# Tap division ahead of the input folds, rotation angles first on ScalarE's queue, batch 1's folds from step 8, ScalarE's side work behind the seed

## The chip, the cores and the metric

The kernel runs on one core of a Trainium2 chip. The metric is the device time of one execution in microseconds; the figure for a kernel is the median of several runs.

## The reference

A Fourier mixing of the input is followed by a gated feed-forward block with a convolution of three taps along the sequence. All is fp32 in effect; the weights come as 8-byte floats.

```
X   = real(fft(fft(x, axis=1), axis=2))          # x: 8 x 3136 x 256
h   = max(X @ w_in, 0)                           # w_in: 256 x 1024
c   = w0 * h[s-1] + w1 * h[s] + w2 * h[s+1]      # conv_w: 3 x 1024, zeros past the ends
out = (h * sigmoid(c)) @ w_out                   # w_out: 1024 x 256
```

## The kernel before

**Setup.** The transform along the sequence uses its symmetries: VectorE folds each batch of x, which comes in two halves (`xh[b, 0]` and `xh[b, 1]`), in eight operations a half (`fold_ops`: `pair(0)`, `pair(2)`, `both(6)`, `feats(1)`, `both(4)`, `turned`, `evens`, `feats(0)`) into the tile w. Part of the odd frequencies is rotated: ScalarE scales by angles in the tile `turn` (`scaled`, L217 for batch 0 and L221 for the others), and for batches 1 to 7 VectorE finishes it (`turned`, L227). For batch 0 the rotated parts are products of their own. TensorE multiplies the folded x by cosine and sine tables (`tabs`, tile tab) in units of one PSUM bank; for each unit ScalarE copies a part (`Unit.copy`, L350, L380, L404) and VectorE combines it (`Unit.fin`). The result is PQ (tiles pt and qt). The transform along the features is multiplied into w_in ahead of time: `blocks` and `column` make G and ge.

The 8-byte weights are narrowed to fp32 by integer operations on VectorE (`narrow`, L618 to L636): conv_w and the first block of w_in at the start, the other blocks of w_in and w_out during the first steps, where a part of it goes to ScalarE (L620).

`taps()` transposes the narrowed conv_w on TensorE, lets ScalarE copy it out of PSUM (L736), and divides the outer taps by the middle one on VectorE (L738 to L744), so that the middle tap needs no product: it is put back as the scale of the sigmoid. In program order it stands right ahead of batch 0's folds.

**Order of the loads.** Loads go out on SyncE's and ScalarE's queues, and the mirrored rows of x by indirect DMAs on POOL (L132). On ScalarE's queue stand conv_w, single rows of x (L126), the four small DMAs of the angles (`load_turn`, L287), and, behind the negation of the angles (L699), one half of the odd tables (L274 to L279). The loads of both queues share eight semaphores in turn, so that each load also waits until the eighth one before it in program order has landed.

**Steps.** After the start the kernel walks through 256 steps (b, c, f): eight batches, four column chunks, eight blocks of 128 of the 1024 columns. The order is written out by hand (`manual_schedule`); all engines take their instructions in that order. In step t:

- ScalarE: `sigmoid` of step t-3 (L835), `copies` of step t+1 (L796), side work listed under "act", `keep`, `seed` of step t+2 (the constant part of h written into PSUM, L760), `first_tap` of t (L811).
- VectorE: `combine` of t (h from two PSUM products, L805), side work "dve", `last_tap` of t-2 (L820), its half of `gate` of t-3 (L844).
- POOL: the other half of `gate` (L843), `middle` of t (an accumulating DMA that adds h to the taps, L815), side work "pool" and the gathers of x under "load".
- TensorE: `products` of t+1 (pb and pa), `mm2` of t-4 (the product with w_out, po), side work "pe".

Side work is put in by `at(step, where, function)`. w_out is narrowed in steps 3, 5, 7 and 9. The features' column sums of batches 1 to 7 are done in steps 11 to 18 (`Feature`: three table operations on ScalarE under "act" in steps 11 to 13, then four stages). The units of batch 1 start at step 21. The 16 fold operations of batch 1 go to the list `cs`, which holds the free steps from 4 on: 4, 6, 8, 10, 11, 12, 13, 14, 16, 17, ... 23. The scaling for the rotation is put into the step of its `turned`, under "act". The loads of batch 2's first half follow batch 1's eighth fold operation.

PE is kept warm by products of no use (`keep_on`, the tile pb at the start) until the tables' products begin.

Of the kernel before, what the change touches and what calls it, by code (L numbers as in the profile page):

```python
# [9 lines left out]
F32 = mybir.dt.float32  # L10
# [3 lines left out]
ALU = mybir.AluOpType  # L14
# [19 lines left out]
TINY = 1e-18  # L34
# [3 lines left out]
def kernel(  # L38
# [10 lines left out]
    nc = tc.nc  # L49
    B, S, D = x.shape  # L50
    F = moe_w_in.shape[1]
    P = 128
# [9 lines left out]
    NF = F // P  # L62
# [6 lines left out]
    const = ctx.enter_context(tc.tile_pool(name="const", bufs=1))  # L69
# [17 lines left out]
    vt = nc.vector.tensor_tensor  # L87
    gt = nc.gpsimd.tensor_tensor
    stt = nc.vector.scalar_tensor_tensor
    act = nc.scalar.activation  # L90

    def mm(o, l, r, start, stop):
        nc.tensor.matmul(o, l, r, start=start, stop=stop, skip_group_check=True)  # L93

    def spare():

        return pso.tile([P, 2, D], F32, name="po", tag="po").rearrange("p a d -> p (a d)")
# [12 lines left out]
    def load_ops(b, h, eng, other=None, held=False):  # L110


        def plain():
            t = xp.tile([P, 8, 2, D], F32, name="xh", tag="xh")
            xh[b, h] = t
            if held:

                nc.gpsimd.memset(t[0:1, 0, 0, 0:1], 0.0)
            eng.dma_start(out=t[0:NP, 0:4], in_=bass.AP(
                tensor=x.tensor, offset=x.offset + (b * S + 1 + 2 * h) * D,  # L120
                ap=[[HQ * D, NP], [Q4 * D, 4], [1, 2 * D]]))

        def zero():
            t = xh[b, h]
            for s0, n, r in ((0, 4, 0), (4, 3, 1), (7, 1, 0)):
                (other or eng).dma_start(out=t[NP:KR, s0:s0 + n], in_=bass.AP(  # L126
                    tensor=x.tensor, offset=x.offset + (b * S + r * Q4) * D,
                    ap=[[D, 1], [Q4 * D, n], [0, 2], [1, D]]))

        def mirrored(m):  # L130
            def f():
                nc.gpsimd.indirect_dma_start(  # L132
                    out=xh[b, h][0:NP, 7 - m].rearrange("p q d -> p (q d)"),
                    out_offset=None,
                    in_=bass.AP(tensor=x.tensor, offset=x.offset,
                                ap=[[2 * D, B * S // 2], [1, 2 * D]]),
                    in_offset=bass.IndirectOffsetOnAxis(ap=idx[0:NP, 0:1], axis=0),
                    element_offset=(b * S + (4 - m) * Q4 - HO + 2 * (1 - h)) * D)
            return f
        return [plain] + [zero] * h + [mirrored(m) for m in range(4)]  # L140
# [142 lines left out]
    def load_turn(eng):  # L283

        for s in range(2):
            for i in range(2):
                eng.dma_start(out=turn[i:NP:2, s].unsqueeze(2), in_=bass.AP(  # L287
                    tensor=dft_seq.tensor, offset=dft_seq.offset + ((2 + s) * NQ + HQ * i) * HE,
                    ap=[[4 * NQ * HE, NP // 2], [2 * HE, 2], [1, 1]]))
# [349 lines left out]
    class Weight:  # L639
# [19 lines left out]
        def narrow(self, c0, c1):  # L659
# [5 lines left out]
    ident = gp.tile([3 * NF, 3 * NF], F32, name="ident", tag="g")  # L665
    make_identity(nc, ident)
    cw24 = gp.tile([3 * NF, 1, P], F32, name="cw24", tag="g")
# [6 lines left out]
           for tag in ("pt", "qt")]  # L674
    w_cv = Weight(cw24, moe_conv_w.rearrange("k (m p) -> (k m) p", m=NF).unsqueeze(1),
                  lambda sh: gp.tile(sh, I32, name="raw", tag="g"))
# [6 lines left out]
    def raw_in(i):  # L683
        def f(sh):
            if i % 2 == 0:
                raws[i // 2] = wp.tile([P, 2, *sh[1:]], I32, name="raw", tag="w%d" % (i // 2))
            return raws[i // 2][:, i % 2]
        return f

    w_in = [Weight(w4[i], moe_w_in[:, i * N4:(i + 1) * N4].rearrange("(t p) n -> p t n", p=P), raw_in(i))  # L690
            for i in range(4)]
    w_cv.load(nc.scalar)
    w_in[0].load(nc.sync)
    for h in range(2):
        for f in load_ops(0, h, nc.sync, nc.scalar, h == 1):
            f()

    load_turn(nc.scalar)
    act(turn[0:NP, 2], turn[0:NP, 1], AF.Copy, scale=-1.0)  # L699
    nc.gpsimd.memset(tabs[0][0:1, 0, 0, 0:1], 0.0)  # L700
    nc.gpsimd.memset(tabs[1][0:1, 1, 0, 0:1], 0.0)
# [7 lines left out]
    wout = const.tile([P, NF, D], F32, name="wout")  # L709
    G = const.tile([P, 2, F], F32, name="G")  # L710
    ge = const.tile([P, NF], F32, name="ge")
    cw = const.tile([P, 3, NF], F32, name="cw")

    def blocks(i):

# [14 lines left out]
                mm(p[:, m:m + 1], w[:, t, m * P:(m + 1) * P], dm[:, t, 1, P - 1:P], t == 0, t == 1)  # L730
        nc.scalar.copy(out=ge[:, i * NF // 4:(i + 1) * NF // 4], in_=p[:, 0:NF // 4])

    def taps():
        p = spare()
        mm(p[:, 0:3 * NF], cw24[:, 0], ident, True, True)
        nc.scalar.copy(out=cw.rearrange("p k m -> p (k m)"), in_=p[:, 0:3 * NF])  # L736
        small = const.tile([P, NF], F32, name="small")
        vt(small, cw[:, 1], cw[:, 1], op=ALU.mult)  # L738
        nc.vector.tensor_scalar(out=small, in0=small, scalar1=TINY * TINY, scalar2=2.0 * TINY, op0=ALU.is_lt,
                                op1=ALU.mult)  # L740
        vt(cw[:, 1], cw[:, 1], small, op=ALU.add)
        nc.vector.reciprocal(out=small, in_=cw[:, 1])
        for k in (0, 2):
            vt(cw[:, k], cw[:, k], small, op=ALU.mult)  # L744


    rows = out.rearrange("b s d -> (b s) d")
# [2 lines left out]
    def cut(s):  # L750
        b, c, f = s
        ch = chunks[c]
        return ch, ch.k1 - ch.k0, slice(f * P, (f + 1) * P)

    def seed(s):

        b, c, f = s
        ch, n, fs = cut(s)
        pa[s] = psa.tile([P, 512], F32, name="pa", tag="pa")
        act(pa[s][:, 0:n], eb[b, c], AF.Copy, scale=ge[:, f:f + 1])  # L760
# [15 lines left out]
    def products(s):  # L776
        b, c, f = s
        ch, n, fs = cut(s)
        pb[s] = psb.tile([P, 512], F32, name="pb", tag="pb")
        mm(pb[s][:, 0:n], G[0:P - 1, 1, fs], PQ[b][1][0:P - 1, ch.k0:ch.k1], True, True)  # L780
        mm(pa[s][:, 0:n], G[:, 0, fs], PQ[b][0][:, ch.k0:ch.k1], False, not triple(s))
        if triple(s):
            mm(pa[s][:, 0:n], G[0:P - 1, 1, fs], PQ[b][1][0:P - 1, ch.k0:ch.k1], False, True)
# [29 lines left out]
    def middle(s):  # L813
        n = gs[s].shape[1]
        nc.gpsimd.dma_start(out=gs[s], in_=hs[s][:, 1:1 + n], accum_op=ALU.add)  # L815
# [15 lines left out]
    def sigmoid(s):  # L831

        v, p, r = shares(s)
        for c in (slice(p.start, r.stop), v):
            act(gs[s][:, c], gs[s][:, c], AF.Sigmoid, scale=cw[:, 1, s[2]:s[2] + 1])  # L835
# [35 lines left out]
        gs.pop(s)  # L871


    w_cv.narrow(0, 1)
    w_in[0].narrow(0, 2)
    taps()
    idle = psb.tile([P, 512], F32, name="pb", tag="pb")

    def keep_on(banks):
# [9 lines left out]
    ops, _, pres = fold_ops(0)  # L889
# [34 lines left out]
    p = psd.tile([P, 512], F32, name="pd", tag="pd")  # L924
# [13 lines left out]
    taken = set()  # L938

    def at(cycle, where, fn):  # L940
        side.setdefault((cycle, where), []).append(fn)
# [16 lines left out]
    ends = [9, 23, per + 12] + [per * (b - 1) - 3 + max(11 - 4 * (b - 2), 0) for b in range(3, B)]  # L958
    def free(cycle):

        while cycle in taken:
            cycle += 1
        taken.add(cycle)
        return cycle
# [13 lines left out]
    for b in range(1, B):  # L978
# [6 lines left out]
        cs = [c0 + i * n // len(us) for i in range(len(us) + 1)]  # L985
        for i, u in enumerate(us):
            k = cs[i + 1] - cs[i]
# [8 lines left out]
    for b in range(1, B):  # L996
        ops, singles, pres = fold_ops(b)
        c0, n = ends[b - 1], ends[b] - ends[b - 1]
        if b == 1:

            cs = [c for c in range(4, ends[1] + 1) if c not in taken]
            assert len(cs) == len(ops) and cs[len(ops) // 2] > NF + 4
        else:
            cs = [free(c0 + j * n // len(ops)) for j in range(len(ops))]
            assert cs[-1] < ends[b]
        if b + 1 < B:
            for h in range(2):
                for j, fn in enumerate(load_ops(b + 1, h, nc.sync)):
                    at(cs[len(ops) // 2 * (h + 1) - 1] + 1 + j, "load", fn)
        for j, fn in enumerate(ops):  # L1010
            at(cs[j], "dve", fn)
        for j, fn in singles.items():
            at(cs[j], "pool", fn)
        for j, fn in pres.items():
            at(cs[j], "act", fn)
# [11 lines left out]
    for t in range(n + LAG):  # L1027
        def run(where):
            for fn in side.get((t, where), []):
                fn()  # L1030
        if 0 <= t - 3 < n:
            sigmoid(steps[t - 3])
        run("first")
        if t + 1 < n:
            products(steps[t + 1])
            copies(steps[t + 1])
        run("act")
        if t >= LAG:
            keep(steps[t - LAG])
        if t < n:  # L1040
            combine(steps[t])
        if t + 2 < n:
            seed(steps[t + 2])
        if t < n:
            first_tap(steps[t])

        run("dve")
        if 0 <= t - 2 < n:
            last_tap(steps[t - 2])
        if 0 <= t - 3 < n:  # L1050
            gate(steps[t - 3])
        if t + 1 < n:
            row_of(steps[t + 1])
        if t < n:
            middle(steps[t])
        run("pool")
        run("load")
        if t >= LAG:
            mm2(steps[t - LAG])
        run("pe")  # L1060
# [66 lines left out]
```

## Time and profile before

| | |
|---|---|
| median of 3 runs | 1190.13 us (1189.02 to 1190.2) |
| the profiled execution | 1192.42 us |
| its span, first to last instruction | 1190.7 us |
| granted TensorE clock, mean | 0.998 |
| PE busy | 1138.7 us (96%) |
| PEld busy | 888.1 us (75%) |
| DVE busy | 957.9 us (80%) |
| ACT busy | 945.0 us (79%) |
| POOL busy | 600.7 us (50%) |

PE is TensorE's matmuls, PEld its weight loads, DVE VectorE, ACT ScalarE, POOL GpSimd, SP SyncE; a q behind the name is the engine's queue of DMA issues and waits. Lines such as L93 are lines of the kernel before; L93 is the helper through which all matmuls go, so these are told apart by their tiles. Matmuls are pipelined and their ends modelled. An idle time is put down to the wait that ended last.

### The profile page before, as it was taken

Reading aid. Unit: us, or ns where it says so; the run is one execution under the profiler, and the core shown is the slowest. Engines: PE = TensorE matmul, PEld = TensorE weight load, DVE = VectorE, ACT = ScalarE, POOL = GpSimd, SP = SyncE. Lnnn points to the kernel's source line nnn. Section 1 sums busy time; section 2 is a strip of 40 time slices with the busy share of each in tenths; the row PEclk is TensorE's granted clock in tenths of the full one; section 3 lists DMA queues with packets and bytes.
Section 4 is the critical chain, followed back from the end, with each engine's and each line's share of the span. In section 5 each row is a group of like instructions: output and inputs, shape, how many; then the busy total and the mean of one; then the engine's idle time right before and its main releaser. Section 6 shows DMA issues by size and latency. Waiting matters only on the chain.

```text
span 1190.7 us, 16046 instructions
## 1 busy us (share of the span) xinstructions
PE 1138.7 (96%) x4818; PEld 888.1 (75%) x4818; DVE 957.9 (80%) x1448; ACT 945.0 (79%) x1939; POOL 600.7 (50%) x734
## 2 busy tenths in 40 slices
PE   0989899999999999999999999999999999999998
PEld 0656678778777787777778777777777777777776
DVE  3689878988788798988787788998787687787774
ACT  0388777887888788888787888888887888898885
POOL 4335765666364546565646464454444444444443
PEclk9999999999999999999999999999999999999999
DMA  7386696767587667767766576765566556666664
GB/s 200 107 153 134 144 161 159 154 139 156 118 193 148 144 122 169 159 149 154 160 137 138 120 173 141 168 142 122 120 124 123 120 121 137 132 131 129 125 122 103
DMA packets 107586, 168.15 MB, mean 141 GB/s; under 512 B 32657, under 2 KB 62627, under 8 KB 107501
## 3 DMA queue, kind: packets, MB, share of 16 engines
q0 software_dynamic: 41984, 115.83, 51.4%
q1 hardware_dynamic: 64345, 50.89, 15.0%
q8 instruction: 38, 0.62, 0.2%
q10 hardware_dynamic: 1172, 0.43, 0.2%
q14 instruction: 47, 0.39, 0.1%
HBM read 38.40 MB, written 25.74 MB: 54 GB/s over the span
## 4 chain that ended last, share of the span: by engine, by line
PE 79%; ACT 7%; DVE 6%; issue 4%; POOL 2%; DMA 2%; ACTq 0%; POOLq 0%; DVEq 0%; SPq 0%
PE po L93 50%; PE pb L93 12%; PE pa L93 11%; PE pd L93 6%; ACT g L835 2%; DVE g L820 2%; ACT nb L796 2%; POOL xh L132 1%; DMA g<-h 1%; ACT os L868 1%; ACT g L811 1%; DMA out_dram<-os 1%; ACT pa L760 1%; DVE xh L168 0%; DVE g L844 0%
## 5 line engine op out<-in xcount | busy, mean ns | idle before, releaser
L93 PE MATMUL po<-wout,g 128*128 128x256 f32 x3072 | 707.2, 380 | 11.1 <-DVE g L844 10.5
L93 PEld LDWEIGHTS po<-wout,g 128*128 128x128 f32 x3072 | 580.1, 190 | 158.2 <-DVE g L844 28.1
L815 POOL DMA_DIRECT2D g<-h x256 | 228.1, 891 | 470.2 <-ACT g L811 244.7
L835 ACT ACTIVATE g<-g,cw 128x385 f32<-128x385 f32 (+2 forms) x512 | 292.0, 623 | 86.6 <-DVE g L820 85.7
L820 DVE SCALAR_TENSOR_TENSOR g<-h,cw,g 128x770 f32<-128x770 f32 (+1 forms) x256 | 299.1, 1168 | 41.7 <-DMA g<-h 41.6
L843 POOL TENSOR_TENSOR g<-g,h 128x385 f32<-128x385 f32 (+1 forms) x256 | 292.7, 1143 | 54.9 <-ACT g L835 53.8
L796 ACT ACTIVATE nb<-pb 128x386 f32<-128x386 f32 (+3 forms) x512 | 226.6, 497 | 93.9 <-PE pb L93 93.3
L805 DVE CUSTOM_DVE_ANT_0 h<-pa,nb 128x386 f32<-128x386 f32 (+3 forms) x512 | 264.2, 556 | 15.7 <-POOL h L774 11.4
L811 ACT ACTIVATE g<-h,cw 128x770 f32<-128x770 f32 (+1 forms) x256 | 244.0, 953 | 0.0
L93 PE MATMUL pb<-qt,G 127*128 127x387 f32 (+2 forms) x512 | 213.9, 499 | 2.3 <-ACT nb L796 1.3
L93 PE MATMUL pa<-pt,G 128*128 128x387 f32 (+2 forms) x512 | 211.9, 494 | 1.7 <-ACT pa L760 1.7
L844 DVE TENSOR_TENSOR g<-g,h 128x385 f32<-128x385 f32 (+1 forms) x256 | 172.9, 675 | 17.9 <-ACT g L835 17.9
L760 ACT ACTIVATE pa<-eb,ge 128x387 f32<-128x387 f32 (+2 forms) x256 | 155.0, 606 | 3.8 <-DVE h L805 3.5
L93 PEld LDWEIGHTS pa<-pt,G 128*128 128x128 f32 x512 | 96.8, 189 | 75.8 <-issue 16.5
L132 POOL DMA_INDIRECT xh<-in_x_dram,idx x64 | 94.8, 1481 | 18.7 <-issue 13.4
L93 PE MATMUL pd<-tab,w 98*128 98x197 f32 (+2 forms) x448 | 98.2, 317 | 1.0 <-POOL w L181 1.0
L93 PEld LDWEIGHTS pb<-qt,G 127*128 127x128 f32 x512 | 90.8, 190 | 8.6 <-ACT nb L796 2.3
L93 PEld LDWEIGHTS pd<-tab,w 98*128 98x128 f32 (+1 forms) x448 | 82.0, 191 | 10.4 <-POOL w L181 1.4
L868 ACT COPY os<-po 128x256 f32<-128x256 f32 x196 | 57.7, 393 | 7.9 <-PE po L93 4.5
L157 DVE TENSOR_TENSOR xh<-xh 98x1020 f32<-98x1020 f32 (+1 forms) x32 | 47.6, 1492 | 0.0
L168 DVE TENSOR_TENSOR xh<-xh 98x1024 f32<-98x1024 f32 (+1 forms) x32 | 44.8, 1400 | 0.1
L227 DVE SCALAR_TENSOR_TENSOR w<-w,turn,rt 98x256 f32<-98x256 f32 x28 | 12.6, 491 | 25.3 <-ACT rt L221 21.3
(140 smaller groups left out, 425.1 us busy)
## 6 DMA issues: line engine op xcount, KB each, us to landing
g<-h POOLq DMA_DIRECT2D x192, 385.0 KB, 4.0
g<-h POOLq DMA_DIRECT2D x64, 416.0 KB, 4.2
out_dram<-os SPq DMA_DIRECT2D x192, 128.0 KB
xh<-in_x_dram SPq DMA_DIRECT2D x16, 784.0 KB
eb<-ed SPq DMA_DIRECT2D x16, 193.5 KB
raw<-in_moe_w_in_dram SPq DMA_DIRECT2D x4, 512.0 KB
raw<-in_moe_w_out_dram SPq DMA_DIRECT2D x1, 2048.0 KB
eb<-ed SPq DMA_DIRECT2D x8, 209.0 KB
```

The costliest lines, as they stand in the source:

```text
L93: nc.tensor.matmul(o, l, r, start=start, stop=stop, skip_group_check=True)
L132: nc.gpsimd.indirect_dma_start(out=xh[b, h][0:NP, 7 - m].rearrange("p q d -> p (q d)"), out_offset=None, in_=bass.AP(tensor=x.tensor, offs ...
L760: act(pa[s][:, 0:n], eb[b, c], AF.Copy, scale=ge[:, f:f + 1])
L796: act(nb[s][:, i, cols], p[:, cols], AF.Copy, scale=-1.0 if i else 1.0)
L805: nc.vector._custom_dve(TENSOR_ADD_SAT, out=to, in0=a[:, cols], in1=c[:, i, cols], s0=BIG, s1=0.0)
L811: act(gs[s], hs[s][:, 0:n], AF.Copy, scale=cw[:, 0, s[2]:s[2] + 1])
L815: nc.gpsimd.dma_start(out=gs[s], in_=hs[s][:, 1:1 + n], accum_op=ALU.add)
L820: stt(out=g, in0=h[:, k:k + n], scalar=cw[:, k, f:f + 1], in1=g, op0=ALU.mult, op1=ALU.add)
L835: act(gs[s][:, c], gs[s][:, c], AF.Sigmoid, scale=cw[:, 1, s[2]:s[2] + 1])
L843: gt(g[:, p], g[:, p], h[:, p], op=ALU.mult)
L844: vt(g[:, v], g[:, v], h[:, v], op=ALU.mult)
L868: nc.scalar.copy(out=osb[:, j % 2], in_=pt[:, j % 2])
```

## The change

Four things are done:

- `load_turn` goes ahead of conv_w on ScalarE's queue, which makes the angles its first load.
- conv_w and the first block of w_in are narrowed and `taps()` is called right behind the first loads. VectorE's and TensorE's order stays as it was (only line numbers move); on ScalarE the copy of the taps now stands ahead of the negation of the angles and of the odd tables' DMAs.
- The 16 fold operations of batch 1 go to a list of steps written out: 8, 10 to 14, 14, 16, 16, 17 to 23. The second half keeps its steps. The POOL copies, the scalings and the loads of batch 2's first half that go with the fold operations move with them.
- In each step `run("act")` moves from ahead of `keep` to behind `seed`, for all batches.

```diff
+    cw = const.tile([P, 3, NF], F32, name="cw")
+
+    def taps():
+        p = spare()
+        mm(p[:, 0:3 * NF], cw24[:, 0], ident, True, True)
+        nc.scalar.copy(out=cw.rearrange("p k m -> p (k m)"), in_=p[:, 0:3 * NF])
...
+    load_turn(nc.scalar)
     w_cv.load(nc.scalar)
     w_in[0].load(nc.sync)
     for h in range(2):
         for f in load_ops(0, h, nc.sync, nc.scalar, h == 1):
             f()
 
-    load_turn(nc.scalar)
+    w_cv.narrow(0, 1)
+    w_in[0].narrow(0, 2)
+    taps()
     act(turn[0:NP, 2], turn[0:NP, 1], AF.Copy, scale=-1.0)
...
-    w_cv.narrow(0, 1)
-    w_in[0].narrow(0, 2)
-    taps()
     idle = psb.tile([P, 512], F32, name="pb", tag="pb")
...
-            cs = [c for c in range(4, ends[1] + 1) if c not in taken]
-            assert len(cs) == len(ops) and cs[len(ops) // 2] > NF + 4
+            cs = [8, 10, 11, 12, 13, 14, 14, 16, 16, 17, 18, 19, 20, 21, 22, 23]
+            assert len(cs) == len(ops) and cs[-1] <= ends[1] and not taken & set(cs)
...
-        run("act")
         if t >= LAG:
             keep(steps[t - LAG])
         if t < n:
             combine(steps[t])
         if t + 2 < n:
             seed(steps[t + 2])
+        run("act")
         if t < n:
             first_tap(steps[t])
```

More of the change, by code (lines that the diff above doesn't have):

```diff
@@ L691 @@
             for i in range(4)]
+    cw = const.tile([P, 3, NF], F32, name="cw")
[3 more added lines that the diff above has]
+        nc.scalar.copy(out=cw.rearrange("p k m -> p (k m)"), in_=p[:, 0:3 * NF])
+        small = const.tile([P, NF], F32, name="small")
+        vt(small, cw[:, 1], cw[:, 1], op=ALU.mult)
+        nc.vector.tensor_scalar(out=small, in0=small, scalar1=TINY * TINY, scalar2=2.0 * TINY, op0=ALU.is_lt,
+                                op1=ALU.mult)
+        vt(cw[:, 1], cw[:, 1], small, op=ALU.add)
+        nc.vector.reciprocal(out=small, in_=cw[:, 1])
+        for k in (0, 2):
+            vt(cw[:, k], cw[:, k], small, op=ALU.mult)
+    load_turn(nc.scalar)
     w_cv.load(nc.scalar)
@@ L711 @@
     ge = const.tile([P, NF], F32, name="ge")
-    cw = const.tile([P, 3, NF], F32, name="cw")
     def blocks(i):
@@ L731, in column @@
         nc.scalar.copy(out=ge[:, i * NF // 4:(i + 1) * NF // 4], in_=p[:, 0:NF // 4])
[L733 to L744, printed above, removed]
     rows = out.rearrange("b s d -> (b s) d")
```

## The prediction

> **What bounds the kernel now.** I read the page first, then the busy time in stretches that follow the kernel's stages, then the waits, then the order of time of the first 42 us and of the first steps. The page's span, and the stretches (length, then PE, PEld, DVE, ACT and POOL busy with instruction counts, granted clock, DMA share, GB/s):
>
> ```profile
> span 1190.7 us, 16046 instructions
> ...
> 0.00:29.10 29.10, 0.59 (x2) 0.53 (x3) 11.10 (x26) 1.67 (x3) 12.47 (x29) 1.00 0.79 197
> 29.10:42.20 13.10, 11.19 (x29) 5.86 (x29) 12.74 (x17) 5.47 (x15) 4.44 (x7) 1.00 0.35 109
> ...
> 81.20:112.00 30.80, 28.09 (x111) 20.85 (x112) 30.59 (x52) 24.48 (x46) 14.87 (x25) 1.00 0.57 111
> 112.00:132.00 20.00, 16.59 (x68) 11.54 (x66) 15.06 (x22) 17.48 (x52) 12.19 (x15) 1.00 0.77 172
> ...
> 500.00:1000.00 500.00, 499.86 (x2128) 395.66 (x2127) 408.12 (x617) 417.46 (x850) 248.32 (x306) 1.00 0.66 138
> ```
>
> From 500 us on TensorE has no idle time. What a schedule can win lies ahead of that: 29 us in which PE does nothing, a stretch to 112 us in which VectorE is full (30.59 of 30.80) and PE is not, and 3.4 us lost by PE between 112 and 132 us. The change touches all three.
>
> Why the first 29 us are empty, in the timeline (start, length, what, idle time before it and its releaser):
>
> ```profile
> 0.75 0.67 ACTq L652 DMA_DIRECT2D raw<-in_moe_conv_w_dram  x1
> ...
> 2.80 0.21 DVE L618 TENSOR_SCALAR cw<-raw 24x128 int32<-24x128 int32 x1 [2.80 <-DMA raw<-in_moe_conv_w_dram]
> ...
> 5.26 5.64 ACTq L287 DMA_DIRECT2D turn<-dft_seq_dram  x4
> 5.26 0.43 DVE L618 TENSOR_SCALAR win<-raw 128x512 int32<-128x512 int32 x1 [0.39 <-DMA raw<-in_moe_w_in_dram]
> ...
> 6.25 0.97 POOL L132 DMA_INDIRECT xh<-in_x_dram,idx  x1 [0.30 <-issue]
> ...
> 11.77 0.97 POOL L132 DMA_INDIRECT xh<-in_x_dram,idx  x1 [0.30 <-issue]
> ...
> 18.30 1.28 ACT L699 ACT_TABLE_LOAD   x1 [18.30 <-DMA turn<-dft_seq_dram]
> ...
> 23.33 0.18 ACT L736 COPY cw<-po 128x24 f32<-128x24 f32 x1 [3.54 <-DMA tab<-dft_seq_dram]
> 23.54 0.17 DVE L738 TENSOR_TENSOR small<-cw 128x8 f32<-128x8 f32 x1 [14.19 <-ACT cw L736]
> ...
> 24.55 2.34 DVE L157 TENSOR_TENSOR xh<-xh 98x1020 f32<-98x1020 f32 x2
> ...
> 26.85 1.63 SPq L652 DMA_DIRECT2D raw<-in_moe_w_in_dram  x3
> ...
> 29.10 7.36 PE L93 MATMUL pb<-w 98*128 98x512 f32 x12 [23.49 <-POOL w L179]
> ...
> 33.25 2.35 DVE L157 TENSOR_TENSOR xh<-xh 99x1020 f32<-99x1020 f32 x2
> ...
> 42.16 0.60 PE L93 MATMUL po<-tab,w 98*128 98x196 f32 x2 [1.91 <-ACT tab L301]
> ```
>
> VectorE is done with the weights at 23.54 - 14.19 = 9.35 and then stands for 14.19 us, not for x but for a 0.18 us copy of the taps. That copy stands on ScalarE behind the negation of the angles (L699), which waits for their load until 18.30, and behind the odd tables' DMAs, which wait again. The folds of x stand behind the taps on VectorE, and PE's real work behind the folds at 42.16.
>
> **The start of the folds.** The angles' four DMAs go first on ScalarE's queue, then the conv weights; the copy now stands ahead of everything that waits for the angles. What the new order waits for is the conv weights' load, no longer first. The answer for the tile turn has the ns of one issue (min/median/max), the one for xh the us from issue to landing of the gathers of x:
>
> ```profile
> L287 ACTq DMA_DIRECT2D turn<-dft_seq_dram x4: 767/774/853, 5.3 to 10.1; - x4
> ```
>
> ```profile
> DMA to landing us min/median/max: 5.4/7.0/8.8
> ```
>
> Four issues of 0.774 put the load's issue at 0.75 + 3.1 = 3.9 instead of 0.75. Its landing is bounded by the quickest and the slowest small load shown: 2.05 us after issue (0.75 to 2.80, engines empty) gives 5.9; the angles' own, from the end of their issues at 5.26 + 5.64 = 10.9 to 18.30, 7.4 us, gives 3.9 + 0.67 + 7.4 = 12.0. I take the gathers' minimum, 5.4, since they are issued into the same traffic of x and w_in: 9.3. Then on VectorE: the taps' narrowing 2.07 (2.80 to 5.26 less the 0.39 idle), w_in's 4.09 (5.26 to 9.35), the division 1.01 (23.54 to 24.55): 7.17. The folds start at 9.3 + 7.2 = 16.5 instead of 24.55, **8.0 us earlier**; by the bounds at 13.1 or 19.2, 11.4 or 5.4 us earlier.
>
> By the Trainium skill's page "DMA: Bandwidth & Descriptors", section "Queues, rings and completion order", each DMA engine changes between its queues after every packet, so that a short load on ScalarE's queue would not stand behind x on SyncE's; that favours the early bound, but the angles' 7.4 us here speak against so quick a turn.
>
> Is x there? The first half's last gather is issued at 6.25 and lands by 6.25 + 5.4 = 11.7 at the earliest, 15.0 by the 8.8; the second half's (11.77 + 7.0 = 18.8) is wanted at 16.5 + 8.7 (24.55 to 33.25) = 25.2. So x hides unless the load takes the early bound. Behind the waiting copy on ScalarE stand the angles' negation and the odd tables' DMAs; these went out after 18.30 and now go at about 12, so nobody waits longer. Each queued load also waits, in the program's order, for the eighth load before it: x's second half now for the first angles' load, its single rows for w_in and the next angles, all early. The folds and the first matmuls hang on each other and move as one. SyncE issued the last table before the row of 26.85; 5.4 on it is there at 32.3, where ScalarE, which mirrors it shortly before PE's 42.16 - 8.0 = 34.2, takes it up. That cover is thin, but SyncE's loads also waited for the late angles and move forward with them. All 8.0 us count.
>
> **Batch 1's folds.** Steps count from the first combine; step 4 is at 81 us, step 12 at 116. Eight fold operations move from steps 4, 6, 8, 10 to 14 onto 8, 10 to 14, 14, 16; the second half stays, so step 16 gets two. With them go two small copies on POOL (10 and 14 to 12 and 16), the scaling on ScalarE (12 to 14) and batch 2's first load on SyncE with its four gathers on POOL (15 to 19 to 17 to 21). Those I cost at nothing, as batch 2's folds begin at step 23 and POOL is busy for 12.19 of 20 us; where POOL lacks that room, a gather (0.97 in the row of 6.25) stands ahead of a tap's DMA and costs a step that much. Steps 3, 5, 7, 9 hold w_out's narrowing. PE's output products in these steps, and the three engines in steps 11 to 13:
>
> ```profile
> 90.07 2.86 PE L93 MATMUL po<-wout,g 128*128 128x256 f32 x12 [0.65 <-DVE g L844]
> ...
> 94.60 2.86 PE L93 MATMUL po<-wout,g 128*128 128x256 f32 x12 [0.38 <-DVE g L844]
> ...
> 99.66 0.70 PE L93 MATMUL po<-wout,g 128*128 128x256 f32 x2 [0.90 <-DVE g L844]
> ...
> 117.22 1.15 ACT L835 ACTIVATE g<-g,cw 128x385 f32<-128x385 f32 x2
> 118.25 0.88 ACT L796 ACTIVATE nb<-pb 128x386 f32<-128x386 f32 x2
> ...
> 120.03 0.89 ACT L221 ACTIVATE rt<-w,turn 98x256 f32<-98x256 f32 x2
> 120.83 0.57 ACT L760 ACTIVATE pa<-eb,ge 128x387 f32<-128x387 f32 x1
> ...
> 121.39 0.88 DVE L227 SCALAR_TENSOR_TENSOR w<-w,turn,rt 98x256 f32<-98x256 f32 x2 [4.05 <-ACT pa L760]
> ...
> 121.45 0.92 PE L93 MATMUL pa<-pt,G 128*128 128x387 f32 x2 [1.35 <-ACT pa L760]
> ...
> 123.73 2.86 PE L93 MATMUL po<-wout,g 128*128 128x256 f32 x12 [1.37 <-DVE g L844]
> ...
> 126.98 1.01 DVE L820 SCALAR_TENSOR_TENSOR g<-h,cw,g 128x770 f32<-128x770 f32 x1
> 127.92 0.55 DVE L844 TENSOR_TENSOR g<-g,h 128x385 f32<-128x385 f32 x1
> ...
> 128.39 1.01 DVE L805 CUSTOM_DVE_ANT_0 h<-pa,nb 128x386 f32<-128x386 f32 x2
> 128.52 2.86 PE L93 MATMUL po<-wout,g 128*128 128x256 f32 x12 [0.62 <-DVE g L844]
> ```
>
> and one step's products that waited for nothing, in the chain of work that ended last (start, length):
>
> ```profile
> 133.59 2.59 PE po L93 x12
> ```
>
> Removed: without folds in steps 4 and 6 VectorE runs ahead by 1.2 us from step 4 (2.34 for two such folds at the start) and by as much again from step 6, and three waits for gates go: 0.65 + 0.38 + 0.90, each with 0.27 for the refilled pipeline (2.86 against 2.59), 2.7 us. In step 12 ScalarE's scaling for the rotation delayed the seed (PE 1.35) and VectorE's rotation (4.05, then PE 1.37): 3.0 with the refill. The 0.62 behind step 13 goes too, as the two operations of that step move on: 0.9. Sum 6.6.
>
> Added: in step 14 the rotation and the two operations behind it share VectorE with the usual combine, last tap and gate, and wait for a scaling that now stands behind the seed. From start to start ScalarE needs for sigmoid 1.03 (117.22 to 118.25), copies 0.8, seed 0.5 (0.57 less the overlap) and scaling 0.8 (120.03 to 120.83), 3.1 us, while VectorE has gate (0.47) and combine (as long as a tap, 0.94), 1.4: it waits 1.7. Its step is combine 0.94 + 1.7 + rotation 0.88 + two operations of 0.68 + tap 0.94 + gate 0.47 = 6.3. PE's is 99.66 - 94.60 - 0.90 - 0.27 = 3.9: 2.4 over, 2.7 with the refill. Step 16, with two of 0.68 and a fold of 1.17: 0.94 + 1.36 + 1.17 + 0.94 + 0.47 = 4.9, 1.0 over. Sum 3.7, net **-2.9**. What isn't shown is how much of step 14's excess PE's lag of four steps absorbs and how long the operations get beside POOL; the answer for line 172 has the 0.68 and the spread (ns min/median/max):
>
> ```profile
> L172 DVE TENSOR_TENSOR xh<-xh x16: 680/1044/1261, 30.7 to 884.0; 98x512 f32<-98x512 f32 x8, 99x512 f32<-99x512 f32 x8
> ```
>
> The same subtraction takes 0.68 alone at the start and up to 1.26 among the steps; two of those add 1.2. So this part lies between -6.6 (all absorbed) and +1.5 (all contended, the early waits half kept). The Trainium skill's page "SBUF — State Buffer", section "Who interferes with whom", has VectorE instructions with two SBUF inputs contend with GpSimd's reads; by it the denser steps 14 and 16 would cost the 1.2 and a little more, and the 1.26 above agrees.
>
> **Side work behind the seed.** In every step with unit copies, feature tables or scalings, the seed goes out earlier and the side work later by one seed. One kind of such wait in the list of waits (total, times, longest):
>
> ```profile
> DVE as L384 <- ACT as L380: 33.2, 15, 6.9
> ```
>
> and PE's output products in the lines from 180 us on (busy, mean ns | idle before and its releasers):
>
> ```profile
> L93 PE MATMUL po<-wout,g 128*128 128x256 f32 x2820 | 648.3, 379 | 4.2 <-DVE g L844 3.7 <-POOL h L774 0.3
> ```
>
> VectorE already stands for these copies, 2.2 us a time in this row, and each such wait grows by a seed, 0.5 to 0.57. There are some 70 (8 units in 7 batches, 14 scalings): 35 to 40 us of VectorE's time, with last tap and gate queued behind each, and PE behind the gate. But after 180 us PE waits for a gate 3.7 us in all, so the growth falls mostly into spare time. I charge **+2.0**; the bounds are 0 and, if a sixth reaches PE, 6.5. Earlier seeds bring nothing after step 12, since PE's idle rows there name gates.
>
> **Sum.** -8.0 - 2.9 + 2.0 = -8.9. The profiled execution took 1192.42 us, 1.7 around its span; it would become 1183.5. It stands 2.3 above the median of 1190.13, so the median goes to **1181.2**.
>
> **Rivals.**
> 1. The conv weights land early. At the quick bound, landing at 5.9, with ScalarE's short load served between packets of x: folds at 13.1, 11.4 us won. 1190.1 - 11.4 - 2.9 + 2.0 = 1177.8. For it: the 2.05; against: the 7.4. Chance 0.12. (The Trainium skill's rule, cited above, leads here.)
> 2. They land late, with x's second half near 18: folds at 25, the start stays, and 1190.1 + 0.6 - 2.9 + 2.0 = 1189.8; no change. For it: it shares the DMA engines with all of x; against: it is 24 rows only and issued ahead of half of x. This is also the case in which the change does not do what it says. Chance 0.06.
> 3. The folds' squeeze: steps 14 to 16 at the +1.5 bound: 1190.1 - 8.0 + 1.5 + 2.0 = 1185.6. For it: VectorE is full there. Chance 0.12.
> 4. Slower: VectorE becomes the bound of the long run, the lengthened waits reaching PE whole. 38 us for all 70: 1190.1 - 8.0 - 2.9 + 38 = 1217. It decides from 22 of them on (10.9 by 0.5). For it: the waits' 2.2 us each; against: PE's idle of 3.7. Chance 0.08.
>
> The forecast has 0.62. The range takes in rivals 1 and 3 and the bounds: at best 1190.1 - 11.4 - 6.6 + 0.5 = 1173, at worst 1190.1 - 5.4 + 0.8 + 2.0 = 1187.5: **1173 to 1187.5**, which leaves out rivals 2 and 4 and little more. A measurement here tells 0.2%, 2.4 us. Faster by more: 0.62 + 0.12 + 0.12 = 0.86; within: 0.06; slower: 0.08.
>
> **What would show it.** Right: VectorE's first fold at about 16.5 us after an idle time of the conv weights' load, PE's first table product near 34; no waits of PE at the gates of steps 5 to 7 and none for the seed of step 12; a new wait at step 14 or 15; VectorE's waits for unit copies longer by half a us with PE full after 180 us. Wrong: a fold start after 19, or PE waits for gates after 180 us well above 4 us.

## The result: slower, and the profile after

The changed kernel takes 1202.86 us (1201.45 to 1203.92) against 1190.16 us for the kernel before on the same chip: a ratio of 1.0104, 95% interval 1.0086 to 1.0122, so 10 to 14.5 us slower. The forecast was 1181.2, and the range of 1173 to 1187.5 doesn't hold the result. The profiled execution took 1203.92 us. Behind line 690 of the kernel before the lines have moved: the copy of the taps is L697 (was L736), the division L699 to L705 (L738 to L744), the copies of pb L801 (L796), the seed L765 (L760), the first tap L816 (L811), the last tap L825 (L820), the sigmoid L840 (L835) and VectorE's half of the gate L849 (L844).

The page after: the chain of work that ended last, by engine.

```profile
PE 69%; ACT 11%; DVE 10%; issue 5%; POOL 2%; DMA 2%; ACTq 0%; DVEq 0%; POOLq 0%; SPq 0%
```

The engines' line of the same part of the page of the kernel before:

```profile
PE 79%; ACT 7%; DVE 6%; issue 4%; POOL 2%; DMA 2%; ACTq 0%; POOLq 0%; DVEq 0%; SPq 0%
```

TensorE lost ten points of the chain, eight of them to ScalarE and VectorE. Where that happened is seen by comparing, step by step, when VectorE's combine starts in the two traces (us, the other kernel less the kernel before, negative is earlier; the labels are those of the experiments below). The profiled execution of the kernel before took 1192.42 us, 2.3 above its median, so every row stands about 2 us too low against the times:

| start of the combine of step | 0 | 8 | 13 | 14 | 15 | 24 | 30 | 80 | 144 | 208 | 255 |
|---|---|---|---|---|---|---|---|---|---|---|---|
| after | -3.7 | -4.7 | -8.3 | -9.7 | -5.5 | -3.5 | -1.4 | +2.8 | +8.3 | +11.1 | +11.5 |
| e1 (side work put back) | -5.5 | -6.6 | -10.7 | -12.0 | -7.4 | -6.9 | -6.9 | -7.7 | -7.0 | -7.1 | -7.1 |
| e2 (side work alone) | -0.6 | -0.6 | -0.1 | -0.5 | -1.6 | -0.1 | +2.1 | +5.5 | +9.9 | +12.6 | +12.9 |
| e4 (list alone) | -0.4 | -1.5 | -5.3 | -6.7 | -2.2 | -2.1 | -2.1 | -2.7 | -2.7 | -2.8 | -2.8 |
| e5 (e1, conv weights first) | -10.3 | -11.3 | -15.0 | -16.3 | -12.1 | -12.4 | -12.4 | -13.7 | -12.9 | -13.2 | -13.2 |
| e8 (after, last tap ahead) | -5.8 | -1.6 | -3.5 | -4.8 | -0.7 | +0.9 | +3.8 | +0.2 | +7.0 | +9.7 | +9.9 |
| e11 (after, copies a step early) | -7.1 | -8.1 | -12.2 | -13.4 | -12.1 | -12.2 | -11.0 | -13.5 | -12.4 | -12.9 | -12.9 |
| e12 (e5, copies a step early) | -13.7 | -14.8 | -18.8 | -20.1 | -19.2 | -18.5 | -18.2 | -22.3 | -21.0 | -21.7 | -21.7 |

The changed kernel gains 3.7 us at the start and 6 more up to step 14, gives 4.2 back in one step, and then loses 17 us between steps 15 and 208, a little in each of many steps. Behind step 208, where hardly any side work on the transform is left, it loses almost nothing more.

The start in the timeline after:

```profile
0.75 4.11 ACTq L287 DMA_DIRECT2D turn<-dft_seq_dram  x4
4.90 1.11 ACTq L652 DMA_DIRECT2D raw<-in_moe_conv_w_dram  x1
...
12.87 1.41 POOL L890 MEMSET qt<- 32x1569 f32 x1
13.05 1.30 DVE L618 TENSOR_SCALAR cw<-raw 24x128 int32<-24x128 int32 x1 [13.05 <-issue]
...
20.87 2.35 DVE L157 TENSOR_TENSOR xh<-xh 98x1020 f32<-98x1020 f32 x2
...
38.48 0.60 PE L93 MATMUL po<-tab,w 98*128 98x196 f32 x2 [1.97 <-ACT tab L301]
```

VectorE starts on the conv weights at 13.05, not at 9.3 (the trace names no landing there, only "issue"); the first folds start at 20.87, not at 16.5 (before: 24.55), and PE's first table product behind the late mirror of the tables at 38.48 (before: 42.16).

Steps 12 to 14, first PE's product that had waited for the seed of step 12, then step 14:

```profile
115.21 0.82 PE L93 MATMUL pa<-pt,G 128*128 128x387 f32 x2
...
123.94 1.03 DVE L227 SCALAR_TENSOR_TENSOR w<-w,turn,rt 98x256 f32<-98x256 f32 x2 [4.20 <-ACT rt L221]
...
127.63 4.54 PE L93 MATMUL po<-wout,g 128*128 128x256 f32 x12 [2.69 <-DVE g L849]
```

PE's wait of 1.35 us for the seed of step 12 is gone, and in its place stands, in step 14, a wait of VectorE for the scaling (4.20) with a wait of PE for the gate behind it (2.69).

The groups of lines from 180 us on, PE's output products (busy, mean ns | idle before and its releasers):

```profile
L93 PE MATMUL po<-wout,g 128*128 128x256 f32 x2792 | 643.5, 380 | 10.8 <-DVE g L849 9.9 <-POOL h L779 0.3
```

9.9 us of waiting for gates instead of 3.7. All of PE's idle time between 180 and 1000 us is 13.0 us instead of 4.2 (807.02 and 815.81 us busy of 820). And the waits of the whole run (who <- whom: total, times, longest):

```profile
ACT g L840 <- DVE g L825: 119.0, 113, 4.2
DVE as L384 <- ACT as L380: 41.8, 15, 6.9
DVE w L227 <- ACT rt L221: 32.8, 14, 4.2
DVE as L354 <- ACT as L350: 29.4, 15, 3.5
DVE as L413 <- ACT as L404: 19.3, 7, 3.4
DVE as L410 <- ACT as L404: 15.0, 7, 2.8
```

In the kernel before, the first of these (there L835 and L820) stood at 85.7, the second at 33.2, the last two at 17.5 and 13.3, and the others at:

```profile
DVE as L354 <- ACT as L350: 23.5, 15, 3.0
DVE w L227 <- ACT rt L221: 21.3, 13, 3.3
```

### The profile page after: what moved, and what is told of

Same layout as the page of the kernel before. It is cut to its first block, busy times and chain, and to the rows that moved or that the text cites. A ratio compares the mean times of both kernels' runs of the same rounds, so it can differ in the third digit from the quotient of the medians.

```text
span 1202.1 us, 16047 instructions
## 1 busy us (share of the span) xinstructions
PE 1145.7 (95%) x4818; PEld 887.3 (74%) x4818; DVE 949.1 (79%) x1448; ACT 943.1 (78%) x1939; POOL 592.3 (49%) x734
## 4 chain that ended last, share of the span: by engine, by line
PE 69%; ACT 11%; DVE 10%; issue 5%; POOL 2%; DMA 2%; ACTq 0%; DVEq 0%; POOLq 0%; SPq 0%
PE po L93 44%; PE pb L93 10%; PE pa L93 10%; PE pd L93 5%; DVE g L825 4%; ACT g L840 3%; ACT nb L801 3%; ACT pa L765 2%; POOL xh L132 1%; ACT g L816 1%; ACT os L873 1%; DVE g L849 1%; DMA out_dram<-os 1%; DMA g<-h 1%; DVE h L810 1%
## 5 line engine op out<-in xcount | busy, mean ns | idle before, releaser
L820 POOL DMA_DIRECT2D g<-h x256 | 227.9, 890 | 470.1 <-ACT g L816 259.0
L840 ACT ACTIVATE g<-g,cw 128x385 f32<-128x385 f32 (+2 forms) x512 | 292.0, 623 | 119.4 <-DVE g L825 119.0
L825 DVE SCALAR_TENSOR_TENSOR g<-h,cw,g 128x770 f32<-128x770 f32 (+1 forms) x256 | 291.9, 1140 | 43.5 <-DMA g<-h 43.4
L848 POOL TENSOR_TENSOR g<-g,h 128x385 f32<-128x385 f32 (+1 forms) x256 | 286.1, 1118 | 77.8 <-ACT g L840 76.0
L801 ACT ACTIVATE nb<-pb 128x386 f32<-128x386 f32 (+3 forms) x512 | 226.2, 496 | 76.8 <-PE pb L93 76.2
L816 ACT ACTIVATE g<-h,cw 128x770 f32<-128x770 f32 (+1 forms) x256 | 244.2, 954 | 0.6 <-ACT ft L552 0.6
L849 DVE TENSOR_TENSOR g<-g,h 128x385 f32<-128x385 f32 (+1 forms) x256 | 175.5, 685 | 20.8 <-ACT g L840 20.7
L765 ACT ACTIVATE pa<-eb,ge 128x387 f32<-128x387 f32 (+2 forms) x256 | 154.2, 602 | 2.8 <-DVE h L810 2.7
L93 PEld LDWEIGHTS pb<-qt,G 127*128 127x128 f32 x512 | 90.7, 190 | 10.5 <-ACT nb L801 4.1
L132 POOL DMA_INDIRECT xh<-in_x_dram,idx x64 | 83.7, 1307 | 18.6 <-issue 13.4
L873 ACT COPY os<-po 128x256 f32<-128x256 f32 x196 | 57.7, 393 | 10.2 <-DMA out_dram<-os 5.7
L168 DVE TENSOR_TENSOR xh<-xh 98x1024 f32<-98x1024 f32 (+1 forms) x32 | 45.4, 1418 | 0.1
L227 DVE SCALAR_TENSOR_TENSOR w<-w,turn,rt 98x256 f32<-98x256 f32 x28 | 13.7, 530 | 32.8 <-ACT rt L221 32.8
```

What stands on the lines that cost most here:

```text
L132: nc.gpsimd.indirect_dma_start(out=xh[b, h][0:NP, 7 - m].rearrange("p q d -> p (q d)"), out_offset=None, in_=bass.AP(tensor=x.tensor, offs ...
L801: act(nb[s][:, i, cols], p[:, cols], AF.Copy, scale=-1.0 if i else 1.0)
L816: act(gs[s], hs[s][:, 0:n], AF.Copy, scale=cw[:, 0, s[2]:s[2] + 1])
L825: stt(out=g, in0=h[:, k:k + n], scalar=cw[:, k, f:f + 1], in1=g, op0=ALU.mult, op1=ALU.add)
L848: gt(g[:, p], g[:, p], h[:, p], op=ALU.mult)
L849: vt(g[:, v], g[:, v], h[:, v], op=ALU.mult)
```

## Experiments

**Which of the parts costs.** e1 is the changed kernel with the side work put back ahead of the seed; e2 is the kernel before with only the side work moved; e3 and e4 are the kernel before with only the start and only the list. The edit of e1, and in reverse of e2:

```diff
             copies(steps[t + 1])
+        run("act")
         if t >= LAG:
...
             seed(steps[t + 2])
-        run("act")
         if t < n:
```

> The changed kernel with ScalarE's side work put back ahead of the seed; the earlier start and the list of fold steps stay. Theory A (the side work behind the seed lengthens VectorE's waits for it and is what costs the time): 1182 to 1188 us, start 3.7 us earlier as in the changed kernel, PE's waits for gates after 180 us back to about 4 us. Theory B (the list of fold steps, with the stall of step 14 and batch 2's later loads, throws the rest out of step): 1198 us or more.

> The kernel before with one edit, the side work behind the seed. Theory A: 1202 to 1208 us, PE's waits for gates after 180 us at 10 us or more. Theory B: 1189 to 1192 us.

> The kernel before with the earlier taps and the angles first on ScalarE's queue alone. Both theories: 1186.4 us, 3.7 us off the first combine and nothing lost later. If the earlier start is given back later whatever else is done: 1190 us.

> The kernel before with the list of fold steps alone. Theory A: 1186 to 1191 us, no loss that grows with the steps. Theory B: 1198 us or more.

Measured, against the kernel before at 1190.27 us:

| | us | ratio, 95% interval |
|---|---|---|
| e1, all but the side work | 1185.52 | 0.9958 [0.9941, 0.9975] |
| e2, the side work alone | 1205.04 | 1.0119 [1.0102, 1.0135] |
| e3, the start alone | 1186.29 | 0.9975 [0.9965, 0.9984] |
| e4, the list alone | 1189.60 | 0.9990 [0.9980, 1.0000] |

In microseconds by the ratios: start -3.0 (-4.2 to -1.9), list -1.2 (-2.4 to 0), side work +14.2 (+12.1 to +16.1). Their sum of +10.0 lies near the +12.4 (10.2 to 14.5) of all together. The side work turns a gain into a loss. PE's output products from 180 us on in e1 and then in e2, from the groups of lines, show the same place:

```profile
L93 PE MATMUL po<-wout,g 128*128 128x256 f32 x2808 | 645.5, 379 | 3.9 <-DVE g L849 3.4 <-POOL h L779 0.3
```

```profile
L93 PE MATMUL po<-wout,g 128*128 128x256 f32 x2792 | 643.4, 380 | 9.3 <-DVE g L844 8.5 <-POOL h L774 0.3
```

**Which of the side work.** The kernel before with only the units' copies (e6), or only the 14 scalings for the rotation (e7), behind the seed. The edit of e6 (in e7 the line of the scalings, `at(cs[j], "act", fn)`, changes in the same way):

```diff
             seed(steps[t + 2])
+        run("act2")
         if t < n:
...
-            at(cs[i + 1], "act", u.copy)
+            at(cs[i + 1], "act2", u.copy)
```

> The kernel before with the 56 unit copies alone moved behind the seed; scalings and feature tables stay ahead of it. Theory A by count, 56 of some 70 waits of the 14.8 us: 1200 to 1203. If the loss comes from the scalings or the feature tables in steps 11 to 18: 1190.

> The kernel before with the 14 scalings for the rotation alone moved behind the seed. By count: 1192 to 1194. If they are what costs: 1200 or more.

e6 took 1199.23 (1.0077 [1.0060, 1.0094]) and e7 1195.23 (1.0044 [1.0032, 1.0055]). Together that is 14.4 us, the whole of e2: both kinds cost, and the 14 scalings cost more apiece (0.37 us) than the 56 units (0.16).

**The order on ScalarE's queue.** e5 is e1 with the conv weights' load first again and the angles' second:

```diff
-    load_turn(nc.scalar)
     w_cv.load(nc.scalar)
+    load_turn(nc.scalar)
```

> The kernel of e1_act_back with the conv weights' load put back to the first place on ScalarE's queue and the angles' four loads second. If the place of the conv weights' load alone sets when the folds start: VectorE has the narrowed weights near 9.4 us as in the kernel before, the taps near 10.5, and folds from where x's first half has landed, 12 us; 8 to 9 us less than e1_act_back, 1176 to 1178. If the tables then come late (the last ones landed by 32 us at the latest by the prediction, and would be taken up at 28): 1179 to 1183.

1178.69 us, 0.9898 [0.9878, 0.9919]: 7 us better than e1. In its timeline:

```profile
0.74 0.67 ACTq L652 DMA_DIRECT2D raw<-in_moe_conv_w_dram  x1
1.45 3.42 ACTq L287 DMA_DIRECT2D turn<-dft_seq_dram  x4
2.93 0.21 DVE L618 TENSOR_SCALAR cw<-raw 24x128 int32<-24x128 int32 x1 [2.93 <-DMA raw<-in_moe_conv_w_dram]
10.06 1.28 ACT L697 ACT_TABLE_LOAD   x1 [10.06 <-DMA xh<-in_x_dram]
...
12.60 2.34 DVE L157 TENSOR_TENSOR xh<-xh 98x1020 f32<-98x1020 f32 x2
```

The weights land 2.2 us after issue and are narrowed before anything else wants VectorE; the folds start at 12.60, now held by ScalarE's copy (11.35), which stands behind the single rows of x. So the gain of the start lay in where `taps()` stands; giving the angles the first place took about half of it away again by the first combines (5.5 us earlier in e1, 10.3 in e5), and more than half by the times.

**The wait as part of a ring.** The chain of work that ended last, in order of time, in the changed kernel (start, length, what):

```profile
192.71 1.01 DVE g L825
...
193.74 0.23 ACT g L840
193.97 0.35 issue
194.32 0.60 ACT g L840
194.92 0.81 ACT nb L801 x2
195.72 0.13 ACT left L856
195.86 0.52 ACT pa L765
196.37 0.26 ACT as L350
...
196.94 0.35 DVE as L356
197.29 0.06 DVE xh L168
197.35 0.99 issue
198.34 1.09 DVE g L825
```

and in the kernel before, about the same steps:

```profile
187.47 2.59 PE po L93 x12
190.06 1.40 PE pd L93 x8
191.46 0.70 PE pb L93 x2
192.16 0.71 PE pa L93 x2
192.87 2.59 PE po L93 x12
...
197.76 2.59 PE po L93 x12
```

Before, the chain is PE alone, 5.40 us from one po to the next and then 4.89. After, PE is not on it. It goes from a last tap on VectorE to the sigmoid of the same step, first in ScalarE's next step, then through the copies, the seed, the unit's copy, and on VectorE through the unit's combine and a fold operation to the next last tap: 192.71 to 198.34, 5.63 us. (The 0.99 of "issue" are no idle time: the fold operation, L168, takes 1.22 us from 197.20 in the timeline.) The sigmoid needs the last tap just ahead of it and the last tap stands behind the unit's combine, so the ring closes within one step, and PE's lag of four steps lies outside it. Without the seed's 0.52 it would be 5.11, between PE's 4.89 and 5.40. In the timeline of the kernel before, where the seed comes behind the unit's copy, the same step takes 5.20 us from last tap to last tap:

```profile
195.07 1.09 DVE L820 SCALAR_TENSOR_TENSOR g<-h,cw,g 128x832 f32<-128x832 f32 x1
...
200.27 1.08 DVE L820 SCALAR_TENSOR_TENSOR g<-h,cw,g 128x832 f32<-128x832 f32 x1
```

Theory L is that this ring sets the time. Theory F is that VectorE is short of time and any work added to it costs. e8 first tried to take the side work out of the ring by putting VectorE's last tap ahead of it:

```diff
-        run("dve")
         if 0 <= t - 2 < n:
             last_tap(steps[t - 2])
+        run("dve")
```

> The changed kernel with one more edit: VectorE does last_tap ahead of its side work, so that neither the next sigmoid nor what follows on ScalarE hangs on the side work's wait for ScalarE. Theory L (the lengthened wait lies on a loop: sigmoid, copies, seed, unit copy on ScalarE, then fin and last tap on VectorE, then the next sigmoid): the loss goes, 1184 to 1192. Theory F (VectorE is simply short of time, and every wait of it costs wherever it stands): 1200 to 1205, as the changed kernel.

1203.21 us, 1.0109 [1.0092, 1.0126], no better than the changed kernel: where theory F put it, and not where L did. Its waits:

```profile
DVE g L825 <- DMA g<-h: 73.4, 74, 5.1
ACT g L840 <- DVE g L825: 16.1, 19, 2.5
```

The sigmoid's wait for the last tap is nearly gone (119.0 in the changed kernel), but the earlier tap now waits for POOL's accumulating DMA (73.4 against 43.4), with everything of VectorE behind it. By the table e8 loses 10.6 us from step 15 on, where the changed kernel loses 17.0. But it also loses 4.2 us between steps 0 and 8, where the changed kernel gains 1.0: PE waits 3.68 us for the narrowing of w_in there, and the granted clock is 0.53 from 71 to 82 us. The mean clock of its four runs is 0.991 to 0.994, against 0.998 in the kernel before; as an estimate, 0.006 of 1200 us is up to 7 of the 13 us that e8 is slower by. So part of the ring's loss went, and as much came in elsewhere; by its time alone the run decides nothing between L and F. The same reordering without the side work's move would have been its control; it was not run.

Three runs that decide more. e9 and e10 are the kernel before with a product on VectorE added that nobody reads, in the 70 steps with a unit's copy or a scaling. They differ in its place alone:

```diff
+    def extra():
+        vt(pad, pad, pad, op=ALU.mult)
...
         run("dve")
+        run("extra")    # e9: between the side work and the last tap
         if 0 <= t - 2 < n:
             last_tap(steps[t - 2])
         if 0 <= t - 3 < n:
             gate(steps[t - 3])
+        run("extra")    # e10 instead: behind the gate
```

> The kernel before, with one product of 128x385 on VectorE that nobody reads (a gate half, about 0.5 us) added in each of the 70 steps with a unit copy or a rotation's scaling, between that side work and the last tap. It gives VectorE the delay of the moved side work without moving anything on ScalarE. Theory L (the delay lies on a ring from last tap to sigmoid, copies, side copy, VectorE's side work and the next last tap): 1202 to 1206, as the side work behind the seed alone. Theory F (VectorE is simply short of time): the same, 1202 to 1206. If the loss came from ScalarE's new order and not from VectorE's delay: 1190 to 1193.

> The same 70 products, but behind VectorE's half of the gate, the last of its work in a step. VectorE's busy time grows as in the run before this one; the path from the side copy to the last tap and the sigmoid does not. Theory L: the extra work falls into the time in which VectorE would wait for the next copies, 1190 to 1195. Theory F: 1202 to 1206, no less than with the product ahead of the last tap.

e9 took 1200.77 (1.0103 [1.0078, 1.0128]), e10 1193.93 (1.0034 [1.0021, 1.0047]). The added product in the groups of lines of e9 and of e10:

```profile
L606 DVE TENSOR_TENSOR pad<-pad 128x385 f32<-128x385 f32 x70 | 44.3, 633 | 0.0
```

```profile
L606 DVE TENSOR_TENSOR pad<-pad 128x385 f32<-128x385 f32 x70 | 38.8, 554 | 0.0
```

About 40 us more work for VectorE costs 12.3 us in the ring by the ratio, and 4.0 us behind it. The median of e9 is only 10.4 above the kernel before, a little less than the 1202 to 1206 expected; one of its four runs, 1207.32 at a granted clock of 0.992, raises the ratio. The product itself is longer in e9's place, 5.5 us in all, which is less than the difference of the two runs. VectorE is not short of time; the place decides. The 4.0 say that the place behind the gate is not wholly free.

e11 leaves the side work behind the seed, but puts each unit's copy (batches 2 to 7) and each scaling one step ahead of VectorE's work on it, so that no wait for them is left in the ring:

```diff
-            k = cs[i + 1] - cs[i]
+            k = max(cs[i + 1] - cs[i] - 1, 1)
...
-            at(cs[i + 1], "act", u.copy)
+            at(cs[i] + k, "act", u.copy)
...
-            at(cs[j], "act", fn)
+            at(cs[j] - 1, "act", fn)
```

> The changed kernel, side work behind the seed, but each unit copy of batches 2 to 7 and each rotation's scaling put one step ahead of VectorE's work on it (a unit's matmuls are packed into one step fewer). VectorE finds the copy done, however late it is in its step. Theory L: the loss of 17 us goes but for batch 1's eight units, 1186 to 1191. If the loss were ScalarE's order itself (copies and first taps later in a step), it stays: 1200 to 1204.

1181.66 us, 0.9933 [0.9918, 0.9948]: 21 us below the changed kernel, and 4.3 below the low end of what theory L expected (its first combine comes 7.1 us earlier than in the kernel before, against 3.7 in the changed kernel, so up to 3.4 of the 21 are the start's). By the table it gains 0.8 us from step 15 on, where the changed kernel loses 17.0, and step 14 costs it 1.3 instead of 4.2, which theory L had not counted on. The five rows of VectorE's waits, 138.3 us in the changed kernel, are 15.5 here, the last two of them (L410 and L413) 1.4 and 1.3:

```profile
DVE as L384 <- ACT as L380: 6.7, 2, 5.2
DVE as L354 <- ACT as L350: 4.1, 3, 1.5
DVE w L227 <- ACT rt L221: 2.0, 3, 1.5
```

ScalarE does the same work in the same order within a step. What cost was that VectorE stood for it.

**A version that beats both.** e12 is e5 with the same early copies and scalings.

> The version with the side work ahead of the seed and the conv weights first on ScalarE's queue (1178.69 us), with the same unit copies and scalings a step early. Theory L: the remaining waits of VectorE for unit copies and scalings, and the stall of step 14 (about 4 us of it on PE's side), leave the ring: 1172 to 1176. If those waits are covered while the side work stands ahead of the seed: 1177 to 1180, no difference; if packing the matmuls costs: up to 1182.

1172.92 us, 0.9858 [0.9843, 0.9872], 17 us below the kernel before. By the table it stands 8.5 us ahead of e5 at the end. 3.4 of these are there at the first combine already, where the two kernels' start is the same and only the granted clock differs (0.89 in e5 from 30 to 60 us, 1.00 in e12). 3.3 come from the stall of step 14, which shrinks from 4.2 us to 0.9, and 1.4 from all the steps behind it. The page's chain is back with PE:

```profile
PE 82%; ACT 5%; DVE 5%; POOL 3%; issue 3%; DMA 2%; DVEq 0%; POOLq 0%; ACTq 0%; SPq 0%
```

So beyond the start the early copies are worth about 5 us, most of it the stall that the new list makes. The waits that the kernel before already had for these copies were nearly hidden behind PE: with the side work ahead of the seed, taking them away in the steps behind 15 gained 1.4 us.

## Why the prediction was wrong

**The side work behind the seed: the step that failed.** The waits grew as described: by about a seed each, from 108.8 us to 138.3 in the five rows. The step that failed is "PE waits for a gate 3.7 us in all, so the growth falls mostly into spare time", which sized the term at +2.0 with an upper bound of 6.5; alone it measured +14.2 (+12.1 to +16.1). A small idle time of PE tells that the ring was no longer than PE's step; it doesn't tell by how much it was shorter. The slack was some tenths of a microsecond at most in the steps with side work (5.11 or 5.20 against 5.40 and 4.89 in the ones shown), and the seed is 0.52. Of each of the 70 seeds two fifths to a half came through (14.2 / 70 = 0.20, and 17.3 / 70 = 0.25 from e1 to the changed kernel). A row of the kernel before hinted at it: PE's weight loads for the output products, which take the gate's tile, waited for it 29 times from 180 us on, mostly without delaying a product. Before and after:

```profile
PEld po L93 <- DVE g L844: 14.5, 29, 1.6
```

```profile
PEld po L93 <- DVE g L849: 30.6, 38, 2.0
```

The range did not hold its own upper bound for this term: its worst case takes +2.0. With 6.5 it would have ended at 1192.0, still below the 1202.86. Rival 4 had the mechanism, waits that reach PE, but with VectorE as the bound and the waits whole (38 us); e10 shows that VectorE isn't the bound, and of the 38 us 14 to 17 arrived. Its chance of 0.08 rested on the same reading of PE's 3.7.

**The start: right in kind, less than half its size.** -8.0 was predicted, -3.0 measured alone (e3). The four issues of the angles and the load's own took until 6.0 instead of 4.6, and VectorE took the weights up at 13.05, past the late bound of 12.0 (in e1 and e3 at 10.5, within the bounds). From the issue that is 8.2 us in the changed kernel and 5.9 in e1, where 5.4 was taken. The terms behind the landing were short as well: the 7.17 us of VectorE's work became 7.8 (13.05 to 20.87), and 8.5 in e1. They were taken from rows in which POOL did nothing that matters to it; here a narrowing operation of 0.21 us took 1.30 (last section). The early landing of rival 1 did not occur in any run with the angles first; with the conv weights first, the 2.05 us on which it rested is what e5 shows again (2.2). The rule of the Trainium skill's page "DMA: Bandwidth & Descriptors", section "Queues, rings and completion order", that queues take turns packet by packet, did not give this small load an early landing; the traces do not tell whether the issue, the turns or the landing itself took the time.

**The list: near in most of its parts, too large in the sum.** -2.9 was predicted, and -1.2 (-2.4 to 0) measured alone, short of rival 3's squeeze of +1.5; -2.8 in e4's profile. In it 6.3 us are gained between steps 4 and 14 (predicted 6.6): 1.1 up to step 8, 3.7 at step 13 with the seed's wait, 1.4 at step 14. 4.5 are lost in step 14 (predicted 3.7 for steps 14 and 16). The gate waits of steps 5 to 7 went only in part, 1.1 of 2.7. The two operations behind the rotation took 0.68 each in step 14 of the changed kernel, not the 1.26 of rival 3. That rival's +1.5 needs half of the whole 6.6 to stay; with half of the early waits alone, as the prediction words it, its terms give about -0.4.

**The signs that were named.** The fold start after 19 and PE's gate waits well above 4 us were both put down as what would make the prediction wrong, and both came. The vanished wait for step 12's seed, the new wait at step 14 and the longer waits for unit copies came as named too; full use of PE after 180 us did not, and PE's first table product came at 38.48, not near 34.

## What to carry to other kernels

An engine's idle time in the trace is no measure of the slack that a change may use up: before an instruction is moved behind another, follow the ring that it lies on (here last tap, sigmoid, copies, side copy, combine, last tap), add up its pieces, and compare with the period of the engine that bounds. If two in-order engines hand work to each other within one step, put the producer a step ahead of its consumer; that removed nine tenths of these waits, and the time fell with them, where shuffling the order within the step in e8 moved a good part of them. And ask of a load whose result heads a chain not whether it is small but whether it is first.

## What the runs showed of the hardware that was not expected

VectorE's integer operations stop beside POOL's memsets. In the changed kernel the narrowing operation L618 begins at 13.05, beside a memset that runs from 12.87 to 14.28, and ends at 14.35, 1.30 us instead of 0.21. In e1 it hits another operation of the same kind:

```profile
12.89 2.11 DVE L622 TENSOR_SCALAR win<-win 128x512 int32<-128x512 int32 x1
...
13.31 1.41 POOL L890 MEMSET qt<- 32x1569 f32 x1
```

It takes 0.43 where nothing is beside it. POOL is held as well: a memset of one element, at 12.33 beside the narrowing operations ahead of this one, took 0.57 us in e1, and 0.09 in the changed kernel. The Trainium skill's page "SBUF — State Buffer", section "Who interferes with whom", says that a tensor_scalar can take a pair of ports that VectorE shares with GpSimd and that the later of the two then stands until the other ends, while a sum of two tensors isn't held by an operation that only writes. The traces agree: in e5 the same memset falls beside the folds, two sums of two tensors, and these take 2.34 us as ever.

The issue of a small load was no constant either: the angles' four took 4.11 us first on the queue, 3.42 behind the conv weights' load, and with the same order as in the changed kernel 3.88 in e1. VectorE's start on one 24-row load in unchanged places differed by 2.5 us between runs (10.5 in e1, 13.05 in the changed kernel), so that a start built on it is known to no better than that.

The granted clock does not stay the same within a run. In the changed kernel it is 0.83 over the 10 us from 125 us, and the output products behind PE's wait of 2.69 us took 4.54 us (shown above) instead of the 2.86 that they take behind shorter waits. In the kernel before it is 0.83 from 40 to 50 us, and 1.00 from 115 to 135 us, with waits of 1.35 and 1.37 us. By these figures such a stretch is worth 1.7 us (0.17 of 10, or 4.54 less 2.86). e5 has two of them at the start (0.89 from 30 to 45 and from 45 to 60 us) and e12, with the same start, none; their first combines lie 3.4 us apart. What sets such a stretch off is not shown.
